# Sharing the start's PSUM copies between ScalarE and VectorE, with a new written-out order, in a Linformer attention and MLP-mixer kernel

## The chip, the cores and the metric

The kernel runs on one core of a Trainium2 chip. The metric is the device time of one execution in microseconds; each version is run several times and the median counts.

The engines are named as the profile does: PE (TensorE, with PEld for its weight loads), DVE (VectorE), ACT (ScalarE), POOL (GpSimd) and SP (SyncE). POOL, SP and ACT also have DMA queues (POOLq, SPq, ACTq). Line numbers (L510) are those of the kernel before.

## The reference

Eight batches, each with 8 heads, 1024 rows and 64 columns per head. Attention in the Linformer form is followed by an MLP mixer:

```python
k_proj = einsum('ks,bhsd->bhkd', E, k)          # 1024 rows of k to 64
v_proj = einsum('ks,bhsd->bhkd', F, v)
scores = q @ k_proj.T / 8
x = softmax(scores) @ v_proj                    # heads side by side: 1024 x 512 per batch
u = x + (relu(x.T @ w_tok1) @ w_tok2).T         # token MLP: 1024 -> 256 -> 1024
out = u + relu(u @ w_ch1) @ w_ch2               # channel MLP: 512 -> 1536 -> 512
```

All inputs and the output are float32.

## The kernel before, in words

**What one batch does.** The loads (`load_heads`, L344) bring pairs of heads of k, v and q from HBM through POOL's DMA queue, which casts them to bf16; the same queue brings the weights. `kv_proj` (L510) multiplies k and v by E and F on PE and copies the result out of PSUM (L523): two heads, four copies of 64x128. In batches 0 and 1 `k_transpose` (L550) turns the projected k on PE, and two copies (L561, L566) put it into `kT`; `q_transpose_pe` (L598) turns two heads of q, and one copy of 128x1024 (L606) puts them into `qT`. From batch 2 on these turns are DMA transposes in SP's queue: `q_transpose` (L579, two for a batch), `k_transpose_dma` (L533, from a tile `kb` that the copies of L523 fill), and `turn_u` (L776) for u. Then come the scores (L614), their exponentials on ACT (L623), the product with v (`attend`, L637), which also gives the sum of the exponentials, and the reciprocal (L649) and the product with it (L654) on DVE. That gives x.

**The MLPs.** The token MLP of batch 0 is `token1_part` (L1053) and `token2_part` (L1085); batch 1 has its own (L704, L728); from batch 2 on it is done with seven block products in place of eight (L868, L984). u of batch 0 is turned by PE (`u_transpose_pe`, L1114) with a copy. The channel MLP is done for 16 half-batches of 512 rows, also as seven block products each: `up_set` (L1173) makes the hidden values in three sets, `down_block` (L1282) brings them back; DVE and ACT form the sums of blocks between them. The results are added to u on DVE (L1322 and others), and `store` (L1316) sends them out. The last half-batch ends in `finish` with adds of 512 and 256 columns (L1364, L1372); only there the stores go through SP's and ACT's queues, otherwise through POOL's:

```python
queue = (nc.sync if sh else nc.scalar) if last else nc.gpsimd
```

**What sets the order.** Every piece of work is a job of a `Planner`. The order of all jobs is a string, `ORDER`: two characters name a job, and the jobs are issued one after the other as the string tells. `pin()` keeps each engine to that order, so an engine that waits for one job holds back all jobs behind it on the same engine, and a queue's DMAs start in this order. `SPOTS` gives each PSUM tile its bank. `FILLS` is a list of places in the order: for each entry a blank matmul of 128x512 on a zero tile (`blank(zero)`, L422) is put ahead of the PE job at that place.

```python
for place, j in enumerate(plan):
    if j.eng == "PE":
        for _ in range(FILLS.count(place)):
            blank(zero)
        pin()
```

Loads and DMA transposes are tied as well: they take turns where the code names it ("loads and transposes take turns"), so that a transpose isn't issued before the load that was put ahead of it.

Of the kernel before, what the change touches and what calls it, by code (L numbers as in the profile page):

```python
# [39 lines left out]
    "HCHrK0HtHLMxK1J-K2HIK4HMEeEiK3HAMzMwK5JyHuHwKCHNK6MyHxKDK7HJHvK9HGKHKFKAHyHzHKH+KGHOK8KJKEHHM+I0I1KK"  # L40
    "KBH-I8I2HPKLI3I9KOHQIAIEICHRKPHSKMKIIDHTM-N1KRIBIFHWN7N3HXN8IGI4N4KNIQNCIINDHUKTKUI6IHHYIRN9KVIJN5IK"
    "KSNAISIYNBKWHVILIMN6KZNEKXNHIZNFKbKaKcIOINNINGNJIVKdNRNSIWNKI7NLKeKfKjIXNMKhIbKgKkNNKnNOKYKlKiKmIaK-"
    "IcNPNQI5KoNTL0KQNWNXITNUL3NVLeIdNYIPIUKqIfNZKpKrL4KtL1NaNbKsLgIgIeN2N0QvNcL6KvNdIjKuNeL7L2KwLiL9IhNf"
    "NgLhLjL5LHNiNhL8LAIkLmNlLnNmLkQwLINjNkQxKxNnLpLBNoNqQzNpIlLJLCNrLqLfKzR1NsLPKyNvNtNwLDNzNuLQLoLFNxLs"
    "LEN+Q-LMR0IiLlLrQyNyO1LwLNHZO2N-K+LRO0LOO4O6LuO5LxLvLtL+LSO8O3O9O7LTLKLyQ+L-OAOBLUOGLzOCM1ODM2R2OEOI"
    "OHLLM0OJM4LVOKM5OLLGLaONM3MCOOOPMDLbLWMGOSOMOTRGMEOQRHLXLcOFOVLYMFMHRBR7OZR9M6OROXImM7RCR8MIRDRERAOa"
    "MJMURLObMKMMM8RFOYMLOdRIMAOcRMMNRJMORQMVRKMPOeMWLdLZR5OnRNOoOgOUROOWMQMSMcOrMdRPRRMRMeRVOpRSOhOjOqOs"
    "RTOkOfRUOiMZRXP3MaOlP4R4MBOuR6M9RWMbRYP5P6OvP7MfOmRZRcMgRaP8RdOxReMTOyPARbOtRfMhRgOwPiMXRhP9PmOzPBMY"
    "O+MjMiPDRiPCR3U+RjPkPEMnPLO-RkRlMkMlPnPFRpPqPMRnMoRmPGRoRqRrV1PNPrRsP1PHPtRuPoRtPuRvRzPTV5V3MpV4R+V2"
    "PJPjRwUzMmPsRxPUPIPpRyP+P0S5R-PvS1PVS2P-S6PlPQS3P2S0PyS8PRS9PzSAQ2PwS4SCS7Q0Q3SBSDSKPOSEPxQ5SLSHSFPK"  # L50
    "PSSISNSPQ6Q1PWQ8SOSGPXPPQGSMSRPYQ4PZPaSSQ9Q7V6U-PeSJV0STPbQHQKPcSWQASXSQPfQIQBQLPgQCQNQEQOQJV9VBSUQM"
    "V7VCVAV8QQQYQPSZQRVGSbQZSVVDVHQaSdQSVLVEVFQgVIQTQUQhVJVMSeVQQWVKVRMqSrSfQiSsVNShVVQdVOVPSaQXScSvVSPd"
    "StSgSiSjVTQDVUQVSwQeSySuVXSkQfVWQFSxSzVYQbSlS-VZVcS+VdVeQjSYSmSnT1TmT2QkVfSoSpVaQcT7VgToQlQnVhVbT0T8"
    "ViQoQmTnSqVjTpTBTqTDVkQpT9TCVpTEQrVlTrVnTATFVqVmTsTuVoVrTvTtVtQsTHT3TGQtTJVsVuTwVvTKTxVwTPTyVzTIVxT+"
    "V+VyTQW5PhQqT-TLW6TzV-W1TNT5TRQuW0TOW2U2W3U0WAU3TUU6W8TVU4TXW4W9WBTMT4U7TWWCW7WKTYU5U9TaWDWEU1UAWFTb"
    "U8WHUCWLTZWGWPWNUDWITSUKWOTcUBTTT6WRWMULUOUMUETeUPUNWSUQTdURTiTfWTUSWQUFUTWWWUWJUcUUTgWVWZWbWaTjWdUW"
    "UVTkWeUdUXUGUeWhWrWfUIUkWsWtWiWvUlWXUJUYWkUaWgUmWcWYWwWyWjX7WlWzUhWuThWmW-WpWnWqUiX8X0XDXBUjUHWoXCWx"
    "W+UnX9XEUoUZUfX1UgUpUbXFXAUrXGXqX2UqXmXJUsXPXHX3XKUvXoXLXNUtXrXsXuY6X5UwXtXIXQXvUuTlY7XRXxY8XnY9YAXy"
    "XXXwXYXMYBXpXOUxXZXzX4X6YDXUYOX+XVYEYPYQX-Y0YCXWYFYRUyXaXSY1YSXbYIYTXTY2XcYUYVYJYgXdYWXeYXXiYKYaY4YM"
    "YbXfXgYhYcXjYGYiYeYYYlYmXhYHYZYLY5Y3YNYfYdYnYwXkYkYoYpYjYqYrYzYtXlYsYuZ2Y+Z3YxYyZ4Z0Z6Y-Z7Z5YvZ1"  # L60
)
SPOTS = (
    "0216767372004241743211210031467364663002714006266137366770745014321020343451242142366575657675676667"
    "7557666576757656767765576102412401523203141541105557565676566757775665675764616706422432141243315012"
    "0141427567656565656666670736756201231505435511212012030665767656565656667360764741251524320415432152"
    "0321575666656665656666461563741340314535104120320312376576665656565666627367460403154103035254241214"
    "35776565656565656666471675605021042104541332150313467"
)
FILLS = (6, 11, 15, 15, 15, 15, 15, 15, 15, 18, 18, 30, 30, 30, 41, 41, 60, 60, 87, 87, 87)
# [19 lines left out]
HWK = 0  # L89
FMAX = 3.4028234663852886e38  # L90


class Job:


    def __init__(self, n, eng, occ, lat, fn, prio):
        self.n, self.eng, self.occ, self.lat, self.fn, self.prio = n, eng, occ, lat, fn, prio
        self.deps, self.next, self.takes, self.banks = set(), [], [], []
        self.start = self.end = None
        self.early = self.behind = False  # L100
        self.mms = 0

# [82 lines left out]
def kernel(  # L185
# [13 lines left out]
    nc = tc.nc  # L199
# [3 lines left out]
    KP = E.shape[0]  # L203
# [123 lines left out]

    def sp(t, fn, **kw):
        return pl.add("DMA", t, t + 2.0, fn, **kw)
# [158 lines left out]
    def kv_proj(b, h0, hn, due, block=False, apart=False):  # L488
# [9 lines left out]
        sides = {"k": (0, k_to, "kb" if block else "kp", ET_sb, k_sb), "v": (KP, v_to, "vb", FT_sb, v_sb)}  # L498

        def side(names):  # L500
            bk = Bank(stream[0], full=False)

            def view(n):
                at = sides[n][0]
                return bank(bk).rearrange("p (h d) -> p h d", d=D)[at : at + KP, 0:hn]

            def mm():
                for si in range(NSI):
                    for n in names:
                        nc.tensor.matmul(  # L510
                            view(n), sides[n][3][:, si, :], sides[n][4][:, hs, si, :],
                            start=(si == 0), stop=(si == NSI - 1),
                        )
# [5 lines left out]
            ).mms = NSI * len(names)  # L519
            for n in names:  # L520
                for i in ((0, 1) if n == "k" else (1, 0)):
                    act(
                        cols, lambda n=n, i=i: nc.scalar.copy(out=sides[n][1][i], in_=view(n)),  # L523
                        writes=[(sides[n][2], i, h) for h in heads], uses=[bk],
# [15 lines left out]
    def k_transpose(h0, hn, due):  # L540
# [7 lines left out]
        def mm():  # L548
# [11 lines left out]
        act(  # L560
            hn * KP, lambda: nc.scalar.copy(out=kT[0:D, hs, 0, :], in_=view()[0:D, 0:hn]),  # L561
            writes=[("kT", 0, h) for h in heads], uses=[bk],
        )
        act(
            hn * KP,
            lambda: nc.scalar.copy(out=kT[D : 2 * D, hs, 1, :], in_=view()[D : 2 * D, 0:hn]),  # L566
# [990 lines left out]
```

## Time and profile before

| | |
|---|---|
| median of 3 runs | 419.5 us (419.3 to 419.77) |
| the profiled execution: its time | 419.51 us |
| its span | 417.7 us (1.8 us of the time lie outside it) |
| mean granted TensorE clock | 0.999 |
| PE busy | 409.2 us, 98% |
| DVE busy | 356.8 us, 85% |
| ACT busy | 229.8 us, 55% |
| POOL busy | 66.7 us, 16% |
| HBM read, written | 59.24 MB, 16.78 MB |

The span is the time from the first to the last instruction or packet on the core. Busy time of PE counts pipelined matmuls from start to modelled end, so 100% busy says that there is always one in flight. The three longest groups of matmuls are L1173 and L1282, the channel MLP's two halves, and they fill most of the span; the chain that ended last is PE for 92%. Shares of busy time are means over the whole span, while the stages differ: the first 24 us load and project, the middle repeats one pattern per half-batch, and the last few us store.

A row of the timeline gives the start, the length of the group, the engine, line, operation, and the tiles out and in; brackets at its end give idle time before it and the work that ended this idle time.

### The profile page before, as it was taken

The numbers are of one execution on the slowest core, as the hardware profiler recorded it, in microseconds if no ns is written. First come the engines' busy times: TensorE is split into PE (matmuls) and PEld (weight loads), VectorE is DVE, ScalarE is ACT, GpSimd is POOL, SyncE is SP. The second block draws the span as 40 slices with busy tenths as digits, with TensorE's granted clock in tenths as the row PEclk, the third lists the DMA queues.
The fourth block names the chain that finished last, engine by engine and source line by source line (L and its number), as shares of the span: only waits on it lengthen the run. The fifth ranks groups of instructions, "written<-read, shape, count | busy, mean of one in ns | idle before, by whom it ended". The sixth has DMA issues, their size and how long they took to land.

```text
span 417.7 us, 9441 instructions
## 1 busy us (share of the span) xinstructions
PE 409.2 (98%) x3843; PEld 348.6 (83%) x3843; DVE 356.8 (85%) x760; ACT 229.8 (55%) x446; POOL 66.7 (16%) x105
## 2 busy tenths in 40 slices
PE   7999999999999999999999999999999999999995
PEld 3589888688888889889898888888798889988884
DVE  2288988999999898898989898998898997988684
ACT  2858984375746456565356645564545555362520
POOL 8544020013000220112001210112101000000100
PEclk9999999999999999999999999999999999999999
DMA  9999999996999888899948896396947411230314
GB/s 166 206 201 206 206 202 186 187 149 113 241 161 189 141 184 175 166 189 174 231 77 153 134 241 150 77 194 114 229 77 202 52 52 52 52 100 2 152 51 153
DMA packets 96812, 62.48 MB, mean 150 GB/s; under 512 B 62080, under 2 KB 92288, under 8 KB 96768
## 3 DMA queue, kind: packets, MB, share of 16 engines
q0 software_dynamic: 35088, 45.09, 54.7%
q1 hardware_dynamic: 61056, 16.00, 22.7%
q10 hardware_dynamic: 624, 0.79, 0.6%
q8 instruction: 30, 0.49, 0.5%
q14 instruction: 14, 0.11, 0.1%
HBM read 59.24 MB, written 16.78 MB: 182 GB/s over the span
## 4 chain that ended last, share of the span: by engine, by line
PE 92%; DMA 3%; ACT 2%; POOL 1%; issue 0%; DVE 0%; POOLq 0%
PE psum L1173 35%; PE psum L1282 34%; PE psum L868 4%; PE psum L984 4%; PE psum L510 3%; PE psum L614 3%; PE psum L673 2%; DMA k_sb<-in_k_dram 1%; DMA kT<-kb 1%; PE psum L637 1%; PE psum L1085 1%; PE psum L1053 1%; PE psum L704 1%; ACT qT L606 1%; PE psum L598 1%; PE psum L1114 0%
## 5 line engine op out<-in xcount | busy, mean ns | idle before, releaser
L1282 PEld LDWEIGHTS <-G 128*128 128x128 bf16 x1344 | 130.5, 98 | 16.8
L1282 PE MATMUL psum<-wc_sb,G 128*128 128x256 bf16 x768 | 103.8, 273 | 0.0
L1173 PEld LDWEIGHTS <-wc_sb 128*128 128x128 bf16 x768 | 73.9, 98 | 10.4 <-issue 0.4
L1282 PE MATMUL psum<-wT,G 128*128 128x256 bf16 x576 | 78.4, 273 | 0.0
L1195 ACT ACTIVATE G<-psum 128x512 bf16<-128x512 f32 x96 | 57.3, 600 | 36.3 <-PE psum L1173 36.2
L1209 DVE TENSOR_TENSOR G<-G 128x512 bf16<-128x512 bf16 (+1 forms) x140 | 69.7, 516 | 1.3 <-ACT a L623 0.5
L1173 PEld LDWEIGHTS <-wT 128*128 128x128 bf16 x576 | 55.5, 98 | 8.5 <-issue 1.0
L1173 PE MATMUL psum<-S,wc_sb 128*128 128x256 bf16 x384 | 57.1, 273 | 0.0
L1173 PE MATMUL psum<-uT,wc_sb 128*128 128x256 bf16 x384 | 56.6, 273 | 0.0
L1173 PE MATMUL psum<-S,wT 128*128 128x256 bf16 x384 | 56.1, 273 | 0.0
L1316 POOL DMA_DIRECT2D out_dram<-o x30 | 16.2, 543 | 204.1 <-DVE o L1322 139.0
L623 ACT ACTIVATE a<-psum 128x512 bf16<-128x512 f32 x64 | 37.2, 601 | 19.0 <-PE psum L614 18.9
L1322 DVE TENSOR_TENSOR o<-psum,u 128x512 f32<-128x512 f32 x59 | 40.4, 685 | 6.8 <-PE psum L1282 6.4
L1201 ACT COPY ub<-psum 128x512 f32<-128x512 f32 x48 | 28.2, 588 | 31.6 <-PE psum L1173 27.7
L1201 ACT COPY ua<-psum 128x512 f32<-128x512 f32 x48 | 28.2, 589 | 21.3 <-PE psum L1173 20.9
L1216 ACT COPY psum<-psum 128x512 f32<-128x512 f32 x48 | 27.8, 580 | 20.2 <-PE psum L1173 9.1
L1154 DVE CUSTOM_DVE_ANT_0 G<-psum,ua 128x512 bf16<-128x512 f32 x48 | 32.9, 685 | 5.3 <-PE psum L1173 2.7
L1154 DVE CUSTOM_DVE_ANT_0 G<-psum,ub 128x512 bf16<-128x512 f32 x48 | 32.9, 686 | 4.8 <-PE psum L1173 4.3
L344 POOL DMA_DIRECT2D v_sb<-in_v_dram x18 | 13.4, 746 | 103.4 <-DMA uT<-u 51.8
L1173 PE MATMUL psum<-uT,wT 128*128 128x256 bf16 x192 | 28.8, 273 | 0.0
L690 DVE TENSOR_TENSOR x_sb<-psum,rdn 128x512 bf16<-128x512 f32 x40 | 27.6, 689 | 0.9
L614 PE MATMUL psum<-qT,kT 128*128 128x512 bf16 x64 | 22.1, 380 | 0.3
(106 smaller groups left out, 546.1 us busy)
## 6 DMA issues: line engine op xcount, KB each, us to landing
out_dram<-o POOLq DMA_DIRECT2D x30, 512.0 KB, 4.5
v_sb<-in_v_dram POOLq DMA_DIRECT2D x14, 512.0 KB, 6.6
k_sb<-in_k_dram POOLq DMA_DIRECT2D x14, 512.0 KB, 8.7
q_sb<-in_q_dram POOLq DMA_DIRECT2D x14, 512.0 KB, 11.4
wc_sb<-in_moe_w_ch_dram POOLq DMA_DIRECT2D x6, 256.0 KB, 12.1
wc_sb<-in_moe_w_ch_dram POOLq DMA_DIRECT2D x4, 384.0 KB, 13.6
k_sb<-in_k_dram POOLq DMA_DIRECT2D x4, 256.0 KB, 7.1
v_sb<-in_v_dram POOLq DMA_DIRECT2D x4, 256.0 KB, 7.0
```

The source lines that it names most:

```text
L614: lambda: nc.tensor.matmul(bank(bk), kT[:, h].rearrange("p c k -> p (c k)"), qT[:, h].rearrange("p j s -> p (j s)"), start=True, stop=True,),
L623: lambda: nc.scalar.activation(out=a_t[h // 2 % 2][:, h % 2], in_=bank(bk), func=ACT.Exp, scale=scale),
L690: lambda: nc.vector.tensor_tensor(out=x_sb[:, :, h * D : (h + 1) * D].rearrange("p (n c) d -> p n c d", n=2), in0=view()[:, :, :, 0:D], in ...
L868: nc.tensor.matmul(to, tok1_of(n, si), mv, start=(n == 1 and si == 0), stop=(si == NJ - 1), skip_group_check=True,)
L1154: nc.vector._custom_dve(TENSOR_ADD_SAT, out=out, in0=in0, in1=in1, s0=FMAX, s1=0.0)
L1173: nc.tensor.matmul(t[:, c, :], w1_of(n, dd, 2 * m + c), a_of(j, n, dd), start=(n in (1, 7) and c == 0 and dd == 0), stop=(c == 1 and dd == 1),
L1195: lambda: nc.scalar.activation(out=G[:, n, cs], in_=view(src), func=ACT.Relu),
L1201: 512, lambda: nc.scalar.copy(out=dst, in_=view("y")), writes=[(name, s % 2)],
L1209: 512 * len(both), lambda: f(out=G[:, n, c], in0=G[:, a, c], in1=G[:, b, c]), ps=False,
L1216: 512, lambda: nc.scalar.copy(out=view("y"), in_=view("x")), takes=[bk["y"]],
L1282: nc.tensor.matmul(to, G[:, G_OF[n], cc, t * P : (t + 1) * P], w2_of(n, cc), start=(n in opens and (t == 0 or alone) and cc == 0), stop=(c ...
L1322: 512, lambda: nc.vector.tensor_add(out=dst, in0=view(src), in1=u_of(sh, dh)),
```

## The change

**Copies.** A helper `copy()` issues a PSUM copy to ACT or to DVE. 29 units of copies (those of a `kv_proj` call, of a `k_transpose`, a `q_transpose_pe` or a `u_transpose_pe` in batches 0 and 1) take their engine from a string `SIDES`, one character each. Five are D: unit 0 (k and v of heads 0 and 1 of batch 0: four copies of 64x128), unit 5 (q of heads 2 and 3: one copy of 128x1024), unit 7 (kT of heads 4 and 5: two copies of 64x128), and in batch 1 unit 22 (kT of heads 0 to 3: two copies of 64x256) and unit 24 (q of heads 2 and 3: one of 128x1024). These ten copies go from ACT to DVE.

```diff
+SIDES = "DAAAADADAAAAAAAAAAAAAADADAAAA"
...
+    sides = iter(enumerate(SIDES + "A" * 99))
+
+    def copy(unit, cols, dst, src, **kw):
+        n, engine = unit
+        if engine == "D":
+            j = dve(cols, lambda: nc.vector.tensor_copy(out=dst, in_=src()), **kw)
+        else:
+            j = act(cols, lambda: nc.scalar.copy(out=dst, in_=src()), **kw)
+        j.unit, j.cols = n, cols
+
+    def scalar():
+        return None, "A"
...
+            unit = scalar() if block else next(sides)
             for n in names:
                 for i in ((0, 1) if n == "k" else (1, 0)):
-                    act(
-                        cols, lambda n=n, i=i: nc.scalar.copy(out=sides[n][1][i], in_=view(n)),
-                        writes=[(sides[n][2], i, h) for h in heads], uses=[bk],
+                    copy(
+                        unit, cols, of[n][1][i], lambda n=n: view(n),
+                        writes=[(of[n][2], i, h) for h in heads], uses=[bk],
                     )
...
+        unit = next(sides)
+        for c in range(2):
+            rows = slice(c * D, (c + 1) * D)
+            copy(
+                unit, hn * KP, kT[rows, hs, c, :], lambda rows=rows: view()[rows, 0:hn],
+                writes=[("kT", c, h) for h in heads], uses=[bk],
+            )
...
-        act(
-            1024, lambda: nc.scalar.copy(out=qT[:, 2 * hp : 2 * hp + 2], in_=view()),
+        copy(
+            next(sides), 1024, qT[:, 2 * hp : 2 * hp + 2], view,
...
-        act(
-            512, lambda: nc.scalar.copy(out=uT_t[i][:, :, hp, :], in_=view()),
+        copy(
+            next(sides), 512, uT_t[i][:, :, hp, :], view,
```

**Order.** `ORDER`, `SPOTS` and `FILLS` are new throughout; the matmuls of the jobs are the same, and the blank matmuls go from 21 to 15.

```diff
-FILLS = (6, 11, 15, 15, 15, 15, 15, 15, 15, 18, 18, 30, 30, 30, 41, 41, 60, 60, 87, 87, 87)
+FILLS = (7, 14, 14, 14, 14, 14, 14, 14, 15, 20, 20, 33, 58, 58, 77)
```

What the new order moves, read from the strings:

- The loads of batch 0 (the number is the pair of heads): before k01, v01, v23, q01, k23, q23, q45, k67, k45, v45, q67, v67; after k01, v23, v01, k23, q01, k67, q23, q45, k45, v45, q67, v67.
- The loads behind them: before v, wc2, wc2, k, wc2, wc2, q; after k, v, then four of wc2, then q.
- On PE two score matmuls that stood ahead of the projection of batch 0's v67 stand behind it. Eight matmuls of `token2_part` move from ahead of the first matmul of L1173 to behind it, and four of `u_transpose_pe` from behind to ahead.
- Batch 2: before, the copies of one projection on ACT were vb, kb, kb, vb; after, kb, kb, vb, vb. Its loads were v, v, k, q, k, q, and are q, v, k, k, q, v. The first store of output was issued some time after them, and is now the next in POOL's queue behind them. SP's order is unchanged: q, q, k, u.
- The end: SP's queue had the last block's row t=1 (the output of the last add), then row t=0, then the store of the other 256 columns; it now has these 256 columns, row t=0, row t=1. ACT's queue had the store of the first add and then that of L1364; it now has them the other way round.

More of the change, by code (lines that the diff above doesn't have):

```diff
@@ new lines @@
+    "1A1S0C1D141p1T2A1g1B181E1Q2B2C1i1F1C151h1k1R1j1a19161b1l2D1n1m1U1c1d1V2E1s1X1q271t1e1r2F0D211W1+1Y1f"
+    "29282H1u0E2G1Z222I1-231v201x2a0F2b1w2V2M2W2J2P1y2S2c2X1z2f2Y2K2Q2R0I0H0G0J2Z2L2g2d2h2k2N2i2O2T2e2U2l"
+    "2t2m2p2j2u2n2q332x342r2o2y2-2v3B302z3C2s2w2+0K35313T320c0Y3U3Q360Z3P0a3l3J373D3R3V3E3W0d0e383K3Z410b"
+    "0N0M0L3m3X3Y3F3p3G393a0O3q3n0g3S3b3c3o3s0h3t3H3r3L3d3f420i3v3A3g3u0f3e3I4h0j4543474k4648443w3x504g49"
+    "3y5x51524A4D4l4m4B4i3h5y5-4E4j534o5z4n4p4C0k4J545+4K3z4F3j4r60564L4s3-554R4H0o0l4u620p57580q614G0m63"
@@ new lines @@
+    "593N4S65645A6N5B666O6P5C4O6R5D4P3i4T6S6Z4q3M676a4Q6Q6W6e6A4U5I3k3+4t696X404I4w686B0n6Y6C6D6E4M6T4V4v"
+    "6f6g5E5J6b3O6U6V6F4N6H6G5M6hAH6I6i4W6c0r5F6d4Y6j6L5G6K4x5N6m4X6k6l4Z6p5K6u6q5P6r4a5Q5L6J6v6n5O6w6s6o"
+    "6tAI4c6x6z6M735a6y5R70745S6+6-A9787571725T5b7B79765U7A7K777H7C5c4dAK5H7LAJ7I7D5i7J7E7N7M7F4y7G5V5W7Q"
+    "7O7R7PAL4+7S5YABAA4-7TAC4e4z7V7U7W5j5X7X5f7Z5gAMANAOAQAP7Y7a5h7e7f4b7c7b7gAT5d7d5l7hAVAXAW7i5mAY5kAh"
+    "7j5Z5nAiAZAb5eAj7pAcAdAa81Ak7l7nAeAmAf7qAnAoAlAg5p7r7t7sAu7u5q827mAvAxAp5oAy7oAw7w85AzB05rA+AqB183Ar"
@@ new lines @@
+    "7vA-86B27x7yAs885tAtBBB5B6B7847-7zB880BCBDB3897+B98J87BEBF8BASBA8ABGB48KBJBM8L8D8N8CBHBKBIBNBL8EBP8M"
+    "8OBSBQBTBRBUBO8P8b7k8Q5u8RBZ8TBVBX8cBWBY8SAU8yBa8UBb90BcBdBe91Bf8+5v8V8W94BgBj959E8FAD8X8zBk92AR9FBh"
+    "Bi979G9HBl9I98EnBn8-8HAF9AEjEk4fBm8Z93Br8d9JBsEr9BEpEq9L8jBo8GAEBp9MBuBwEo8k8Y96AGBvByEs8gBxBt999OBz"
+    "Bq5s9WB+C4B-9C9P8lElC08h9XC59a9D8iC1C2C38eC79Y8m9K8aC88n8I9N9ZC68oC9CB8f9Q9bCC8p9R9dCE9cCD8q8uCG9e9g"
+    "8rCN9hCA9fE-Cb8vCF9iCHExCJCOF0CLEzEyCREvE+8s8wEmF4F59oCSF19pCP5w9S9jCM9qCUF2CVF9F3CQCcF69w9k9UCK8tF7"
@@ new lines @@
+    "F8CX9xFA9l9yFBCdCYCfFECtCTFC9mFDFG9tCeFFFOCICuEw9VCvFHFICWCg9u9vFPCxCZCiFJ9zCwFLFKDW9TCa9+CjFM9rCyCz"
+    "FNEuEt9n9-DYFQFRChFS9sC+FTCkFUFVClC-CnD0A1D1A0FWCmD2DXDaD3IoFXFYDbA2CoA5FZD4D9FdDcFbFeDeDdFfA3CpFcFg"
+    "IrA4InDfFiCqFaIvFjDhFhDiDZFkD5IsDAA6DBD7A7CrD6ItFlFnFmDkFoFpFvDlFrFqFsFwDgDHDjFtIuFxF+DoFyF-FzDpDmDn"
+    "CsG8DE8xA8G0FuG1D8DsDFIpIwDqG2DGDtG9DrDIDvE4G5DwG3DJG4DKDyG6GBDLDuGDGAE5GCDMG7E8DxGEDzDCGFD+DOGGDDE9"
+    "DPD-GHGKEBGIDNJ8J9DQGLEAGRGJE0J3J1ECEDE6DSJ4GSE7I-EGJ0EEIqEHGNJ2GPDTEFGTEMDUJ5GUGVJ6GWJ7GOENJDE1GQJA"
@@ new lines @@
+    "GYIzGfGMEOEIJBEUGZJCEKGgJEGbEVJFE2JGJIJHEWGjGcERJJJKJLGkGXJSJTJMGmGlDRGhESEJGaHbGnETJPGpJQGdGiJRGoGx"
+    "JNEXJUGeJVJWELJOGyEYEPE3EZGzJXJYG-EQG+JZGqH0HeGrHaEbJaGsEcHcH2HfHiH1HjJbHdEaJcHgJhEdJdHlH3JeJfJgHmJi"
+    "EfH5EgJjJlH6HhJkH4HkJmHDHnJnH7HqEhH8JrJoHEJpJsHsJqGtHoJvHtHpJzGuH9HrJ+HFJtDVMsIxIyMrI+EeMvJuHBJwHAJx"
+    "K2K0HwHCHLHuJ-JyK1MtMxMzHxK3HzK4GvK5KCMuHMHIHvH+KDI0K6HNGwMyMwK9I1KAM+K7HJKFKGK8I8KHHGKJKEHKHHI9KKHO"
+    "HyKIKLICIAKOH-IDHPKPIBIFKMKBN7N3I2IGHQIIHSHRN4KNI3N8NCN5HTKVIEN6IJKSKRN9KWI4HWHUKTIHIQNAIKKXIRKUNBNE"
@@ new lines @@
+    "ILIMNDNFISKZHXNHNGKaKYIOI6NJHYIYKbIVINN1I5NKKcHVEiIZIWNLIaIXIPNINMKjNOKdNPKfKkHZNQIbKlKQI7KgNNKeKmNT"
+    "ITNWKnKhNUNVNXKoNYIcLeNRKiNSIUKqK-IdNZIfKrL0NaNbNcKtKpL3NdNeL1IgIeN2KsLfKvNfL2L4LHL6NgNlKwNhLIKuM-N0"
+    "QwNjIhL7L9IjNkLgL5NmIkLiQyL8NiIiNnLBNpNoNqLCNrLALDLELFKxKzLjLJQzNsNvLPLmNwQ+Q-LnR1IlNtLQLMLpLkNuR0Ll"
+    "O1LqLGKyLRNxLoLwK+NzN+LNNyN-O3O2LhR2O4O6LrLOO5LxLyL+LuO7O0O8O9LvL-LsLSOAM1LTOBLzM2OCODQvOGM4OHLKOJLL"
+    "OEOILtM5LUImMCOKQxLVONOOM0MDOLLWOPMGMHOMLaM3OSRBOQLXOTORLYRCRGRHR7OFOVM6LbMJMELcR8MIRDR9OZMFM7MKOaMU"
@@ new lines @@
+    "OXREMMM8RAOWRFMLOdObMVMOMNOeOYMAR4R5RLRIOcMPRJMWOnRKOUOgMcMQRMOoRNLZR6MSOhR3MdOrOjM9RVMZMTRORPRSRWMe"
+    "OpMaRTOsRUP3LdUzMbOuRXRQRYMBOqRZMfOfMgOkP4OvRaP5OiRROxOlMRRbRcMXP7MhPiRdOmReP8MjOtP6RfRgMkPAMYOyPmRh"
+    "OwPjMiRiOzRjPBPDPEMnPLMoPnRkPkMlRlP9PqPlO+RpPCO-RnRoPrRqV1PFRmRrPMPGV2V3RsU+PNPtRuPHP1PoPuRvMpRtRwPs"
+    "RzPJPTP2PpRxR+V5PUP+RyV4R-S5PvV6U-V0S1PyS2PVS0P-S3P0Q0PIPwS6S8PzS9SAMmPQSKQ2SBS4SCPRS7PxQ3SLSDQ1QGPS"
+    "Q5SFQ6SEPWSNSHQHSGQ8PKSIQ4SPQ9SOPXPOSRSMPPQ7PYSSQKQIQAQLSTSWQJSQPaQNSUQOPbSXPZQBV7SVSJVGVBPeSZQMV8VH"
@@ new lines @@
+    "VDPcQPQYQQVCVEPfVFQCSbV9QSVLPgQTQRVAQZVMVISaSdSrVQQaSeQgVRVJVKVNMqShSfVVQhSiQUQEVOSgVPPdVSQWQFSsVTSY"
+    "QiQdSkQeSlVWVUSvVXSxSjQVQfVYQDStSwVZQjSySmVcScVdTmSuSpSqQkSzQbT7SnSoQXT8VeS+VfQcQlVgT1QnVhQmT2ToVaTB"
+    "T9T3QoVbTCViS-T0TATqTEQpVjVkVlQrTDT4TFTrVpVqQsVnVmTuTvVrTsQtTHTxVoVtTGVsTnVuTITyVvTtT5TJTwVwVzU2VxTP"
+    "TKTpPhQuU3TLV+TzU6VyQqU4V-W1U7W2TNTMW3W0W5U5TQU9W6WAU0TRUAW8T+WBW9W7TUU1WCT-TXU8TVUCWDWFWETWUDWGW4UK"
+    "TYULTSWKWHTaTZTOUBUOWLT6WITbWNUEWMTTUPURTcWOTdWRWSWPTeUFUMTfTiUNWQUSUQTjUUUcWTUGWJUVTgUTWZWdUWWUWWWr"
@@ L64 @@
[L64 to L67, printed above, removed]
+    "2724114217403233244062631342166077027031640162031764367273645204310510123414223420467676657656777655"
+    "6755676755677565656565766130210231205534414313030775566775667575556777567570757627420142215235410152"
@@ L68 @@
+    "1421256766656565656566665546706300431403413410234502120767667656565656666270672640431543143551254401"
+    "2035577665656565656667260762734112104303124521052032166566765656566666617076474051435051343203520502"
+    "15767567656565676666474761734550332404245132135010467"
 )
[L69 removed]
+FILLS = (7, 14, 14, 14, 14, 14, 14, 14, 15, 20, 20, 33, 58, 58, 77)
 WHOLE = 3
@@ L101, in __init__ @@
         self.mms = 0
+        self.unit = None
 class Bank:
@@ L497, in kv_proj @@
         v_to = [vb[i * KP : (i + 1) * KP, hs, i, 0:D] for i in range(2)]
-        sides = {"k": (0, k_to, "kb" if block else "kp", ET_sb, k_sb), "v": (KP, v_to, "vb", FT_sb, v_sb)}
+        of = {"k": (0, k_to, "kb" if block else "kp", ET_sb, k_sb), "v": (KP, v_to, "vb", FT_sb, v_sb)}
         def side(names):
@@ L510, in mm @@
                         nc.tensor.matmul(
-                            view(n), sides[n][3][:, si, :], sides[n][4][:, hs, si, :],
+                            view(n), of[n][3][:, si, :], of[n][4][:, hs, si, :],
                             start=(si == 0), stop=(si == NSI - 1),
@@ L559, in k_transpose @@
         )
-        act(
-            hn * KP, lambda: nc.scalar.copy(out=kT[0:D, hs, 0, :], in_=view()[0:D, 0:hn]),
-            writes=[("kT", 0, h) for h in heads], uses=[bk],
-        )
-        act(
-            hn * KP,
-            lambda: nc.scalar.copy(out=kT[D : 2 * D, hs, 1, :], in_=view()[D : 2 * D, 0:hn]),
-            writes=[("kT", 1, h) for h in heads], uses=[bk],
-        )
+        unit = next(sides)
[5 more added lines that the diff above has]
+            )
     turned_u, rest = {}, {}
```

55 lines of the change are left out of this document (6 added, 49 removed).

## The prediction

> **What bounds the kernel now.** I read the page's busy table first, then the table of windows, then the waits, the chain and the timeline where a window showed a gap. Line numbers are those of the kernel before.
>
> ```profile
> span 417.7 us, 9441 instructions
> PE 409.2 (98%) x3843; PEld 348.6 (83%) x3843; DVE 356.8 (85%) x760; ACT 229.8 (55%) x446; POOL 66.7 (16%) x105
> 12.00:14.00 2.00, 2.00 (x21) 0.97 (x16) 0.00 (x0) 1.72 (x6) 0.88 (x2) 1.00 1.23 203
> 16.00:18.00 2.00, 1.68 (x15) 0.86 (x17) 0.00 (x0) 2.00 (x5) 1.13 (x2) 1.00 1.23 203
> 20.00:22.00 2.00, 1.91 (x14) 0.84 (x13) 1.65 (x7) 1.96 (x5) 0.55 (x2) 1.00 1.14 210
> 24.00:26.00 2.00, 2.00 (x39) 2.00 (x37) 1.97 (x9) 0.40 (x1) 0.74 (x1) 1.00 1.26 197
> 100.00:150.00 50.00, 50.00 (x466) 43.74 (x464) 47.20 (x96) 27.75 (x54) 8.00 (x13) 1.00 1.04 184
> ```
>
> The columns behind the length are busy time of PE, PEld, DVE, ACT and POOL, then granted clock, DMA share and GB/s. From 24 us on PE has work without a gap (50.00 of 50 us). A time can change in three places only: ahead of 24 us, at a wait inside the full part, and behind the last matmul. Ahead of 24 us ACT is the full engine (2.00 and 1.96 of 2 us) and DVE is empty until 18; PE's weight loads fill under half. So the span is a start that ACT and the loads set, then PE's work, then a tail.
>
> ```profile
> 20.75 0.10 PEld L614 LDWEIGHTS <-kT 128*128 128x128 bf16 x1 [0.48 <-ACT kT L566]
> 22.30 0.63 PE L510 MATMUL psum<-v_sb,EFT_sb 128*64 128x128 bf16 x8
> L344 POOL DMA_DIRECT2D v_sb<-in_v_dram x1: 718/718/718, 10.5 to 10.5; - x1
> DMA to landing us min/median/max: 10.9/10.9/10.9
> ```
>
> These are the timeline, and the issue of the v load for heads 6 and 7. The v data, the last input that batch 0 needs, landed at 10.5 + 10.9 = 21.4. Its projection on PE (L510) began at 22.30, 0.9 later, because PE is in order and what stood ahead of it had waited for ACT's kT copies. PE is full behind it.
>
> **The start.** Five of the 29 copy units go to DVE. In batch 0 that takes from ACT four 64x128 copies at 0.262 (L523), one 128x1024 at 1.012 (L606) and two 64x128 at 0.260 (L561, L566): 1.05 + 1.01 + 0.52 = 2.6 us. ACT was full there, so what waits for ACT comes earlier, up to the next limit: the last v load. It keeps its place among the twelve loads, which only change places, so it lands at 21.4 again. A load that landed at 11.48 had its first matmul at 11.53; so the last projection can begin at 21.42 instead of 22.30: -0.88. The order has two score matmuls less ahead of this projection; they are done behind it and cost 2 x 0.216 = 0.43 there. Sure is then -0.45. Behind 22.3 PE lost another 0.15 to 0.27 in small waits, part of which ACT's lead removes; I take **-0.6**, ends -0.45 and -0.86. Two loads cap it: the third wc2 load lands at 45.37 and the first down products need it at work that PE reached at 46.0 (0.6 to spare); batch 1's q lands at 49.82 for work reached at 50.49. Nothing beyond 0.6 gets past 50 us unless these come earlier; their queue is full, 1.14 to 1.26 in the DMA column of the windows above.
>
> The copies' price on DVE is in no row. A 128x512 eviction on DVE took 0.69 (L451), a 128x256 one 0.42 (L654), a 128x4 one 0.18 (L649): by a straight line 0.30 for 64x128 and 1.23 for 128x1024 (ends 0.26 and 0.42; 0.69 and 1.4). Six and one make 3.0 us, at most 3.9. DVE idles 7.3 us before 14.5 and 3.9 before 19.0, so I cost them at nothing; behind such a copy only reciprocals and products of attend (L649, L654) are queued on DVE, which wait for the same heads anyway. Without that cover one 1.2 us copy would hold attend's outputs, and the token products that read them, for 1.2 us. Batch 1's three copies (two 64x256, one 128x1024; 2.1 us) come near 50 us, where PE waits for neither engine: nothing, 2.1 at worst.
>
> Six blank matmuls go (L422, 6 x 0.217 = 1.3 us). Each stood ahead of a job that waited, so what goes is filler time: nothing, or -0.2 where one delayed its job. The reordered PE jobs of the full part are the same matmuls: nothing.
>
> **The wait at 83 us.**
>
> ```profile
> 77.33 0.58 ACT kb L523
> 77.92 0.58 ACT kb L523
> 78.53 5.10 DMA kT<-kb
> 83.68 0.60 PE psum L614 x2
> ...
> DMA packets 600, 0.60 MB, mean 199 GB/s; under 512 B 16, under 2 KB 600, under 8 KB 600
> q0 software_dynamic: 600, 0.60, 122.7%
> qT<-q_sb SPq DMA_TRANSPOSE x1, 8.6
> ```
>
> First the chain of waits: batch 2's scores waited for the transpose of kb, 5.10 us from issue to landing; 0.38 of it stopped PE (83.30 to 83.68). Then the DMA view of 69 to 72 us: a transpose was issued at 69.00, and all 600 packets belong to queue 0, the loads; transposes moved only once it was empty, at 72.8. In the changed kernel the kb copies go ahead of the vb copies on ACT (1.2 us earlier), the k loads sit earlier, and the first out store (data ready near 64) is queued right behind the last load instead of at 74.56, where it lay among the transposes until 81.5. On SP the order stays qT, qT, kT, uT. Sum: queue empty 72.8, the store 0.524 MB at 0.39 MB/us (rate at 205 to 206) 1.3, so 74.1; two qT of 2.8 and 2.5 (undisturbed ones): 79.4; kT 1.25 and 0.6 to land: **81.3**. The upper end is 83.6, as before. By its matmul list PE wants it 0.2 us earlier in its work, and with the start's 0.6 at 82.5. Midway, 82.45, leaves about 0.1 of the 0.38: **-0.3**, ends -0.38 and +0.7. uT behind it lands at 84.3 to 84.7 (u ready at 80.0, 4.24 to 4.64 in quiet cases) for use at about 85.2: no wait, half a microsecond of cover.
>
> A rule is the other way. The Trainium skill, "DMA: Bandwidth & Descriptors", section "Queues, rings and completion order", says each DMA engine takes turns between its queues packet by packet. By that rule the transposes would share with the store and kT lands like before; the rows at 69 to 72 disagree, those at 78 to 81.5, where packets interleaved, agree.
>
> **The tail.**
>
> ```profile
> 411.52 1.69 ACTq L1316 DMA_DIRECT2D out_dram<-o  x2
> 412.76 0.42 DVE L1372 TENSOR_TENSOR o<-psum,o 128x256 f32<-128x256 f32 x1
> 413.21 1.35 SPq L1316 DMA_DIRECT2D out_dram<-o  x3
> 414.00:415.00 1.00, 0.00 (x0) 0.00 (x0) 0.00 (x0) 0.00 (x0) 0.00 (x0) 1.00 1.04 339
> ```
>
> SP's first store waits for the last add (L1372, to 413.2), and two stores whose data is ready before (409.8, 411.9) stand behind it, issued at 413.63 and 414.12; the last landed at 416.74. About 786 KB leave at 340 GB/s at the very end. In the changed order SP stores the 262 KB piece (ready 409.8) and the t=0 row (131 KB) first, and only t=1 waits. On ACT the two 262 KB stores are swapped against their data: the one ready at 411.5 now stands behind the one ready at 412.8. The burst is 786 - 393 + 262 = 655 KB: 131 / 340 = **-0.4**. Ends: -1.3 if one store issued at 413.2 lands in 2.20 (the quickest of SP's three) and is the last; 0 if the burst's length is not in its bytes. No row speaks for a loss, as nothing is issued later than 414.12.
>
> **Sum.** -0.6 - 0.3 - 0.4 = -1.3. Against the profiled execution's 419.5 (span 417.7, 1.8 outside it), which is the median of the runs too: **418.2**. The likeliest case's own range is 417.3 to 418.7.
>
> **Rivals.**
> *The gain is eaten at 83 us.* If kT lands at 83.6 again, PE only arrives earlier and waits longer; start and wait together give nothing, and the tail alone remains: 419.1, or 419.5 without it. For it: the interleaved packets of 78 to 81.5, and the store that is put ahead of the transposes. Against it: the 1.2 us that kb is earlier. Chance 0.25.
> *The clock falls.* Six blanks less leave PE emptier between 8 and 22 us. The price is in the first blanks:
>
> ```profile
> 0.99 1.03 PE L422 MATMUL psum<-zero 128*128 128x512 bf16 x2 [0.99 <-DVE zero L299]
> 8.12 1.69 PE L422 MATMUL psum<-zero 128*128 128x512 bf16 x7
> ```
>
> Two blanks in a row begin 0.40 apart at the opening (2 in 1.03 us with a 0.6 us tail), 0.217 at 8 us; the slow pace held until about 4.7 us, 3.8 us in all, so one fall costs 3.8 x (1 - 0.217/0.40) = 1.7 us, two 3.4. From 418.2 that is 419.9 to 421.6: slower at its middle, 420.8. It decides if the filling of 16 to 18, the emptiest window, falls by two blanks from 1.68 to 1.25 of 2 us and the clock does not bear it. Against it: that window had 1.00, with gaps under 0.5 us. Chance 0.10. The Trainium skill, "TensorE: Matmul & The Clock Gate", section "A second HAM failure mode: psum-queue depth-cycling", reports a kernel whose short idles between matmul groups made the clock swing; this trace, at 0.999 with such idles, does not show it so far.
> *A later stall.* The order is new everywhere, and a bank or transpose that comes late behind 90 us would stop PE; before there is none. One of 2.5 us gives 420.7. For it: DVE is 94% busy there (47.20 of 50). Against it: the same work in the same time per batch. Chance 0.07.
> *It does not do what it says:* ACT's swapped stores. It is inside the tail's ends.
>
> **How the numbers follow.** The forecast 0.58; eaten gain 0.25; clock 0.10; later stall 0.07. About 0.2% (0.84 us) is what a measurement of this kernel can tell from no change, so faster means under 418.7: the forecast's range, 0.58. The eaten gain is the same, 0.25; clock and stall are slower, 0.17. The range that leaves 2 in 10 out goes from the low end of the sum, 417.3, over the eaten gain to the mildest fall of the clock: 420.1.
>
> **What would show it.** Right: the last v projection at 21.4, the first up product near 31.2 instead of 32.0 (0.6, and 0.2 to 0.3 of token matmuls that its order puts behind it), clock 1.00 in all windows from 8 us, kT landed by 82.5, last matmul near 411.5, SP's stores issued one by one with the last at 412.3, span near 416.4. Wrong: a projection past 22, a wait for DVE in front of a PE instruction before 24 us, a wait of 1 us or more at 82 to 84, a granted clock under 1, any PE gap behind 90.

## The result, and the profile after

The changed kernel took 418.94 us in the median of 22 runs (418.33 to 420.4), the kernel before 419.81 (419.08 to 422.54). The ratio on record is 0.9972, 95% interval 0.9959 to 0.9984: faster by 0.28%, or 1.2 us. The two medians alone give 0.9979, or 0.9 us.

The profiled execution lost 1.1 us of span, 416.6 against 417.7. First the page's head and the table of windows (columns as before: length, busy time of PE, PEld, DVE, ACT, POOL, granted clock, DMA share, GB/s):

```profile
span 416.6 us, 9427 instructions
12.00:14.00 2.00, 1.33 (x15) 0.85 (x13) 0.00 (x0) 1.67 (x5) 0.92 (x2) 1.00 1.24 205
16.00:18.00 2.00, 1.66 (x15) 0.80 (x15) 1.46 (x7) 1.91 (x4) 1.16 (x2) 1.00 1.26 211
20.00:22.00 2.00, 1.80 (x23) 1.42 (x24) 1.43 (x8) 1.43 (x3) 1.08 (x2) 1.00 1.13 211
100.00:150.00 50.00, 49.98 (x464) 43.38 (x463) 46.74 (x97) 28.77 (x55) 6.88 (x11) 1.00 1.03 184
```

ACT has room at 20 to 22 us (1.43 in place of 1.96), DVE works where it was empty (1.46 at 16 to 18), PE has more idle time (it has six blanks less), and the clock is the same. Next the start's timeline and the issue of the last v load (lines shift: L525 is the old L510, L651 the old L637; the copies now carry the helper's lines, L335 on DVE and L337 on ACT):

```profile
20.14 0.62 PE L612 MATMUL psum<-ident,q_sb 128*128 128x128 bf16 x8 [0.76 <-DMA q_sb<-in_q_dram]
20.80 1.01 ACT L337 COPY qT<-psum 128x1024 bf16<-128x1024 bf16 x1 [0.57 <-PE psum L612]
21.47 0.63 PE L525 MATMUL psum<-v_sb,EFT_sb 128*64 128x128 bf16 x8
22.36 0.23 PEld L651 LDWEIGHTS <-a 128*128 128x128 bf16 x4 [0.24 <-ACT a L637]
22.85 0.23 PEld L651 LDWEIGHTS <-a 128*128 128x128 bf16 x4 [0.21 <-ACT a L637]
...
L359 POOL DMA_DIRECT2D v_sb<-in_v_dram x1: 716/716/716, 10.5 to 10.5; - x1
DMA to landing us min/median/max: 10.9/10.9/10.9
```

The v load landed at 21.4 as before, and its projection began at 21.47, not 22.30. Two things are new. Ahead of the projection PE now waits 0.76 us for the load of q heads 6 and 7, which it turns first. Behind it, twice PE waits for an exponential, which ACT makes after the copy of q heads 6 and 7. Then batch 2's transpose and the chain:

```profile
L549 SPq DMA_TRANSPOSE kT<-kb x1: 1352/1352/1352, 77.6 to 77.6; - x1
DMA to landing us min/median/max: 3.3/3.3/3.3
```

```profile
82.77 0.43 PE psum L628 x2
```

kT landed at 80.8; the scores at 82.77 follow PE's own work without a wait. Last the tail:

```profile
409.59 3.28 SPq L1330 DMA_DIRECT2D out_dram<-o  x3
412.08 0.42 DVE L1386 TENSOR_TENSOR o<-psum,o 128x256 f32<-128x256 f32 x1
412.15 0.92 ACTq L1330 DMA_DIRECT2D out_dram<-o  x2
```

SP's stores go out one by one from 409.6. ACT's two stores start only behind the 512-column add; the one whose data had been ready at 410.8 was issued second, at 412.58, and landed last of all, at 415.63.

From one profile to the next the same loads land up to 1.4 us apart, so stretches are compared, not times of day. In us; a star marks a granted clock under 1.00 in the start:

| kernel | v load lands | projection behind it | to the first up product | from there to the last matmul | last add's end to last landing |
|---|---|---|---|---|---|
| before | 21.37 | 0.93 | 9.72 | 380.42 | 3.55 |
| before, second profile | 21.49 | 1.41 | 9.71 | 380.09 | 3.54 |
| before, kb first | 22.09 | 1.06 | 9.68 | 380.07 | 3.55 |
| before, store late | 21.22 | 1.24 | 9.73 | 386.54 | 3.56 |
| before's order, copies shared * | 21.82 | 3.20 | 9.79 | 379.90 | 3.56 |
| changed | 21.37 | 0.09 | 10.07 | 380.23 | 3.13 |
| changed, ACT's stores in data order | 21.40 | 0.17 | 10.10 | 380.23 | 2.82 |
| changed, tail as before | 21.37 | 0.10 | 10.12 | 380.22 | 3.86 |
| changed, one blank * | 20.78 | 0.73 | 10.06 | 380.33 | 3.12 |
| changed, all on ACT * | 21.11 | 3.42 | 9.71 | 380.98 | 3.15 |
| changed, batch 1 on ACT | 21.66 | 0.10 | 10.09 | 380.95 | 3.53 |
| changed, vb first | 21.53 | 0.75 | 10.10 | 380.23 | 3.11 |
| changed, q67 on DVE * | 21.84 | 0.64 | 9.69 | 380.22 | 3.12 |
| the last but with the stores in data order | 21.43 | 0.26 | 9.66 | 380.23 | 2.41 |

Between the two orders 0.27 us of PE work changes sides of the first up product (eight matmuls of `token2_part` at 0.062 go behind it, four of `u_transpose_pe` at 0.056 ahead). At equal work the third stretch is 0.27 longer and the fourth 0.27 shorter in the changed order than the table says. So the pair's 1.1 us are 0.21 ahead of the first up product, 0.46 from there to the last matmul and 0.42 in the tail.

The table measures the projection from the v load, but another load holds it in the new order. The load of q heads 6 and 7 landed at 20.10 in the changed kernel; PE turned these heads, worked on without a gap, and began the projection 1.37 us after that landing. In all six profiles of the new order without a star this distance is 1.37, while the distance from the v load goes from 0.09 to 0.75. The run "vb first" tells the two loads apart: v landed at 21.53, q at 20.91, and the projection kept to q.

```profile
20.96 0.62 PE L612 MATMUL psum<-ident,q_sb 128*128 128x128 bf16 x8 [0.55 <-DMA q_sb<-in_q_dram]
22.28 0.63 PE L525 MATMUL psum<-v_sb,EFT_sb 128*64 128x128 bf16 x8
```

### The profile page after: what moved, and what is told of

It reads as the page before. It is cut to its first block, busy times and chain, and to the rows that moved or that the text cites. A ratio compares the mean times of both kernels' runs of the same rounds, so it can differ in the third digit from the quotient of the medians.

```text
span 416.6 us, 9427 instructions
## 1 busy us (share of the span) xinstructions
PE 407.9 (98%) x3829; PEld 348.3 (84%) x3837; DVE 359.1 (86%) x770; ACT 228.9 (55%) x436; POOL 66.7 (16%) x105
## 4 chain that ended last, share of the span: by engine, by line
PE 92%; DMA 3%; POOL 2%; ACT 1%; DVE 1%; issue 0%; POOLq 0%
PE psum L1187 35%; PE psum L1296 35%; PE psum L998 4%; PE psum L882 4%; PE psum L525 3%; PE psum L628 3%; DMA q_sb<-in_q_dram 3%; PE psum L687 2%; PE psum L651 1%; PE psum L1099 1%; PE psum L1067 1%; PE psum L718 1%; PE psum L742 1%; POOL k_sb L359 1%; PE psum L612 1%; POOL q_sb L359 1%
## 5 line engine op out<-in xcount | busy, mean ns | idle before, releaser
L637 ACT ACTIVATE a<-psum 128x512 bf16<-128x512 f32 x64 | 36.7, 597 | 25.5 <-PE psum L628 21.3
L628 PE MATMUL psum<-qT,kT 128*128 128x512 bf16 x58 | 20.5, 379 | 0.1
```

The lines of the kernel that those rows point to most:

```text
L628: lambda: nc.tensor.matmul(bank(bk), kT[:, h].rearrange("p c k -> p (c k)"), qT[:, h].rearrange("p j s -> p (j s)"), start=True, stop=True,),
L637: lambda: nc.scalar.activation(out=a_t[h // 2 % 2][:, h % 2], in_=bank(bk), func=ACT.Exp, scale=scale),
```

## The experiments

**The copies and the order apart.** Two kernels complete a square.

```diff
-SIDES = "DAAAADADAAAAAAAAAAAAAADADAAAA"
+SIDES = "AAAAAAAAAAAAAAAAAAAAAAAAAAAAA"
```

> The changed kernel's order with all 29 copy units on ACT. Theory (ACT's 2.6 us of relief lets the last v projection start when its load lands): without it the projection of v heads 6 and 7 slips from 21.47 to 22.3 or later, and what follows it on ACT slips too; span +0.5 to +1.5. Rival (the new order and the new order of the loads did it, the copies are beside the path): projection by 21.7, span +0.0 to +0.2.

```diff
 SIDES as in the changed kernel
-ORDER, SPOTS, FILLS of the changed kernel
+ORDER, SPOTS, FILLS of the kernel before
```

> The order, banks and blank matmuls of the kernel before, with the five copy units on DVE: the copies alone. Theory (ACT's relief frees the start): the projection of v heads 6 and 7 goes from 22.30 to 21.5 to 21.9, as the old order has two score matmuls more ahead of it, the wait at 83 us grows or stays, span 417.0 to 417.5 against 417.7. Rival (the copies pay only with an order that is made for them): projection at 22.2 to 22.4, span 417.6 to 417.8.

| ratio to the kernel before | copies on ACT | five units on DVE |
|---|---|---|
| old order | 1 | 1.0011 (0.9996 to 1.0027) |
| new order | 1.0053 (1.0033 to 1.0073) | 0.9972 (0.9959 to 0.9984) |

Neither part gains alone; the new order without the copies loses 0.5%. With all copies on ACT the projection came 3.42 behind its load, more than the theory had. The windows and waits of that run show ACT full and PE empty (the rows of PEld and PE see the same two waits):

```profile
16.00:18.00 2.00, 0.73 (x10) 0.56 (x10) 0.00 (x0) 1.94 (x6) 1.30 (x2) 1.00 1.24 204
18.00:20.00 2.00, 1.68 (x12) 0.85 (x11) 0.98 (x5) 1.99 (x5) 0.74 (x1) 0.65 1.26 210
```

```profile
PEld L651 <- ACT a L637: 2.7, 2, 2.2
PE psum L651 <- ACT a L637: 2.3, 2, 2.0
```

The copies alone did not bring the projection to 21.5: it began 3.2 behind its load, after one wait for DVE's kT copies (1.28 us in PEld's row, 1.02 in PE's). The timeline of that run shows why:

```profile
22.74 0.42 DVE L668 TENSOR_TENSOR x_sb<-psum,rdn 128x256 bf16<-128x256 f32 x1
23.08 0.58 DVE L335 CAST kT<-psum 64x128 bf16<-64x128 f32 x2
23.71 0.10 PEld L628 LDWEIGHTS <-kT 128*128 128x128 bf16 x1 [1.28 <-DVE kT L335]
```

In the old order the copies stand behind attend's products, while the scores (L628) wait for them. My theory of this run was wrong and its rival right. The clock had fallen as well (0.50 at 14 to 16 us), and this execution, 421.86 us, is one of two of ten near 421.9; the other eight took 419.8 to 420.6. So part of the 3.2 belongs to the execution and not to the copies. No run takes the new order apart beyond batch 2's copies, the tail and the blanks: what its new order of loads is worth alone stays open.

**Batch 1's copies.**

```diff
-SIDES = "DAAAADADAAAAAAAAAAAAAADADAAAA"
+SIDES = "DAAAADADAAAAAAAAAAAAAAAAAAAAA"
```

> The changed kernel with batch 1's three copies (kT of heads 0 to 3, q of heads 2 and 3) on ACT again and batch 0's on DVE. Theory of the prediction (these are beside the path): PE waits for no copy between 45 and 60 and works there as in the changed kernel. Rival, from the run with all copies on ACT (PE waited 0.7 and 0.5 at 45 to 60): these copies hold PE there, 0.5 to 0.8 more idle time of PE in 40 to 60 us.

```profile
PEld L1296 <- issue: 0.7, 1, 0.7
PE psum L628 <- ACT a L637: 0.5, 1, 0.5
```

The rival. These waits at 40 to 60 us are absent from the changed kernel, and the stretch to the last matmul was 380.95, 0.72 longer than in the changed kernel. The run with all copies on ACT has the same (380.98). The two rows are one stop of PE, at 54.69, and each kernel has one profile here.

**The blanks and the clock.**

```diff
-FILLS = (7, 14, 14, 14, 14, 14, 14, 14, 15, 20, 20, 33, 58, 58, 77)
+FILLS = (7,)
```

> The changed kernel with one blank matmul in place of 15 in the start (14 x 0.217 = 3.0 us less PE work before 20 us). Theory (the blanks keep the granted clock, and the change came close to losing it): PE runs slow for a time in 8 to 22 us, granted clock under 1 there, two neighbouring 128x512 matmuls 0.4 apart in place of 0.217, span +1.7 to +3.4. Rival (the clock holds with the loads' own matmuls): clock 1.00 and span within 0.2 of the changed kernel, perhaps 0.1 better.

```profile
8.00:10.00 2.00, 0.64 (x15) 0.47 (x15) 0.05 (x1) 0.00 (x0) 2.00 (x4) 0.91 1.20 188
10.00:12.00 2.00, 1.07 (x16) 0.82 (x15) 1.02 (x4) 0.43 (x3) 1.03 (x3) 0.50 1.16 183
```

The clock did fall, to 0.50 from 10 to 16 us; eight transposes of q took 1.04 there, 0.62 in the changed kernel. The mean granted clock of all nine runs is 0.988 to 0.992, so it fell in each. But the price was far under the theory's: the ratio was 0.9975 (0.9966 to 0.9985), which isn't told from 0.9972. The projection began at 21.52, against 21.47 in the changed kernel; it stood 0.73 behind its load, but that load had landed 0.6 earlier, so the 0.73 isn't shown to be the clock's. PE waits for loads in this stretch anyway; that slow matmuls use up this time is my reading, not a measurement.

**The wait at 83 us.**

```diff
 ORDER of the kernel before (two characters a job; 4b is the first store of output)
-AY 4b 5e Aj Ai 7b AZ Aa Ab 7p 5n AC 7q 81 Ae 5p AT 7l
+AY 5e Aj Ai 7b AZ Aa Ab 7p 5n AC 7q 81 Ae 5p AT 4b 7l
```

> The kernel before with the first store of output put behind the next load in POOL's queue, so that it isn't among batch 2's transposes. Theory (its packets among the transposes made kT late): kT lands 3.0 to 3.3 after its issue at 78.5, so by 82, and PE's wait of 0.38 at 83.3 is gone. Rival (kT was late because the kb copies came late or the q transposes ahead of it were long): kT's issue and the wait stay as they were.

kT landed 3.04 after its issue at 78.66 and no wait was left, as the theory had it. The move cost 6 us elsewhere: the store now landed at 93.89, and until then an add (L1332) could not write into its tile, which made PE wait 4.7 us further on. Behind this wait the granted clock fell to 0.50, from 95.9 to 99.3 us. Two rows of the waits and one of the windows:

```profile
DVE o L1332 <- DMA out_dram<-o: 5.0, 1, 5.0
PE psum L1173 <- DVE S L799: 4.7, 1, 4.7
96.00:98.00 2.00, 2.00 (x12) 1.51 (x11) 1.97 (x7) 0.00 (x0) 0.00 (x0) 0.50 0.97 211
```

```diff
 ORDER of the kernel before (AM, AN: kb copies; AP, AO: vb copies)
-AP 5j 7W 5X 7T 7X AM 7U AN 7Y AO
+AM AN AP 5j 7W 5X 7T 7X 7U 7Y AO
```

> The kernel before with the two kb copies of batch 2 ahead of the vb copies on ACT. Theory (the store among the transposes is the cause): kb is ready 0.6 earlier, but SP is busy issuing the q transposes until 78.43, so kT is issued 0.1 earlier at most and PE still waits 0.25 to 0.4 at 83.3. Rival (late kb copies are the cause): the wait is gone.

The wait was gone, against my theory. But the whole start of this execution was 0.8 later, so PE came to the scores at 84.19, and kT landed 3.28 after its issue at 78.70. A second profile of the kernel before itself changed the question:

> The kernel before once more, for a second profile: the loads landed up to 0.9 us earlier or later from one execution to the next. What belongs to the kernel recurs: the last v projection 0.9 to 1.1 behind its load's landing, PE's wait for kT of 0.2 to 0.4 near 83, the last landing 3.5 to 3.6 behind the last add. What belongs to that execution does not.

```profile
L533 SPq DMA_TRANSPOSE kT<-kb x1: 1231/1231/1231, 79.1 to 79.1; - x1
DMA to landing us min/median/max: 3.6/3.6/3.6
```

What I expected to recur did so for the start (1.41, more than my 0.9 to 1.1) and the tail (3.54), not for this wait: kT took 3.6 us in place of 5.1, and PE did not wait. The 0.38 belonged to one execution. That the wait was absent from the two single runs above therefore shows no cause, neither the store's nor the copies'.

```diff
 ORDER of the changed kernel
-AM AN AO AQ AP
+AO AP AM AN AQ
```

> The changed kernel with batch 2's vb copies ahead of its kb copies on ACT. Theory (the store ahead of the transposes gave the time): kT is issued at 78.7 in place of 77.55 and lands 3.3 later, at 82.0, still ahead of the 82.77 at which PE wants it: no wait. Rival (the order of the kb copies took the wait away): PE waits for kT, 0.2 or more, at 82 to 84.

kT was issued at 79.60 and landed at 82.75, and PE did not wait; this execution ran 0.8 later from the start, so PE came to the scores at 83.46. With the vb copies first the new order has no wait either.

**The tail.**

```diff
 ORDER of the changed kernel (Y-, Z1: ACT's two stores; Yv, Z5, Z7: SP's three)
-Yy Z4 Y+ Z0 Z1 Z3 Yv Z5 Z6 Y- Xl Z7
+Yy Z4 Y+ Z0 Z3 Z6 Xl Y- Z7 Z5 Yv Z1
```

> The changed kernel with the five stores of the last half-batch in the order of the kernel before (SP: row t=1, row t=0, the 256 columns; ACT: first add, then that of the 512-column add). Theory (the share of the tail in the gain is the later burst): the last landing goes back from 3.13 us behind the last add to 3.56, span 417.0, +0.4. Rival (the tail's gain came from elsewhere, for example from the last adds): span 416.6 as it is.

Span 417.4, last landing 3.86 behind the last add, ratio 0.998 (0.9963 to 0.9996). By these profiles the order of the stores is worth 0.43 to 0.73 us, by the medians of the runs 0.37 (419.31 against 418.94), and the two intervals overlap. Its size isn't settled: with the changed kernel's stores in the changed kernel's order the run with batch 1 on ACT has 3.53 in the table, and two profiles of one and the same end further down have 2.82 and 2.41. Why it is 3.86 here and 3.54 to 3.56 in all profiles of the old order stays open.

```diff
 ORDER of the changed kernel
-Yy Z4 Y+ Z0 Z1 Z3 Yv Z5 Z6 Y- Xl Z7
+Yy Y- Z4 Y+ Z0 Z1 Z3 Yv Z5 Z6 Xl Z7
```

> The changed kernel with ACT's last two stores in the order in which their data comes. In the changed kernel's trace the store put behind the other (256 columns by two rows, 262 KB, data ready at 410.8) is issued at 412.58 and lands last, at 415.63; SP's last store lands at 414.75. Theory (the queue order holds a ready store back, and that store ends the kernel): it is issued near 410.8 and lands near 413.2, SP's last 131 KB then end the kernel at 414.4 to 414.8, span 415.4 to 415.8 instead of 416.6. Rival (the end is a fixed latency behind the last add, whatever is queued): last landing stays near 415.6, span 416.5 to 416.7.

The early store landed at 413.23, and SP's last store ended the kernel; but that store took 2.79 us to land in place of 2.22, so only 0.3 of the expected 0.8 to 1.2 came: 2.82 behind the last add, span 416.4, ratio 0.9964 (0.9952 to 0.9977), not told from the changed kernel's.

**One more copy on DVE, and both edits.**

```diff
-SIDES = "DAAAADADAAAAAAAAAAAAAADADAAAA"
+SIDES = "DAAAADADAAAADAAAAAAAAADADAAAA"
```

> The changed kernel with one more copy on DVE: that of q heads 6 and 7 (128x1024; 1.01 us on ACT at 20.80, 0.68 on DVE). In the changed kernel PE waited 1.0 us in all for the exponentials between 22 and 24, and ACT does this copy ahead of them. Theory (this copy is what holds the exponentials): they start 0.4 to 0.5 earlier, the first up product comes 0.2 to 0.5 earlier than 31.53, span 416.1 to 416.4. Rival (DVE's reciprocals and products queue behind the copy and hold the token products): first up product at 31.5 or later, span 416.6 to 417.

The stretch from the projection to the first up product was 9.69 in place of 10.07, as the theory had it, and one wait of 0.2 for an exponential was left. The span, 417.4, was no better: the v load landed 0.5 later, and the clock had fallen to 0.50 at 12 to 14 us, though up to 20 us this program is that of the changed kernel. Ratio 0.9969 (0.9957 to 0.9981), not told from the changed kernel's.

> The changed kernel with ACT's last two stores in the order of their data and the copy of q heads 6 and 7 on DVE: both edits that shortened a stretch. From the two runs apart: the last landing came 2.79 behind the last store's issue and 2.37 behind the last add's end in the first (3.13 in the changed kernel), and the stretch from the last v projection to the first up product was 9.70 in the second (10.07). If they add up: first up product 9.6 to 9.8 behind the projection, span end 0.2 to 0.5 earlier behind the last matmul than in the changed kernel, ratio to the kernel before 0.9945 to 0.9965. Rival (either only moved a wait): ratio as the changed kernel's, 0.997.

Both edits together: 417.59 us, ratio 0.9947 (0.9933 to 0.996), span 415.7. First up product 9.66 behind the projection, last landing 2.41 behind the last add (2.82 in the run with the same stores, so 0.4 of it is one execution against another). All five runs, 417.46 to 417.91, lie under the fastest of the changed kernel's 22, 418.33: this version beats both kernels.

## Why the prediction was right or wrong, by its own steps

The sum was -1.3 and the ratio gives -1.2 (-0.7 to -1.7); the forecast case, a gain, came about. The time itself, 418.94, lies above that case's own range (417.3 to 418.7), as the kernel before also took 0.3 more than in its first three runs. The terms hold less well than the sum: at equal work the pair gives -0.21, -0.46 and -0.42 for the forecast -0.6, -0.3 and -0.4. That a start sized too large and a middle sized too small partly cancel is luck.

**The start (-0.6).** Right: with ACT's relief the projection came 0.83 earlier, and two scores went behind it. Right by luck: the place, 21.47 for the predicted 21.42. The prediction named the last v load as the next limit; it was the load of q heads 6 and 7, which landed 1.37 us ahead of the projection in every profile of the new order without a star, and in the first of them this came to 0.09 behind the v load. In "vb first" it came to 0.75. Wrong: "small waits, part of which ACT's lead removes". New waits came there instead, for exponentials queued behind the copy of q heads 6 and 7; the run with that copy on DVE took them away (10.07 to 9.69). In the profiled pair the first up product came 0.48 earlier, 0.21 at equal work, a third of the 0.6. Over all profiles without a star the old order's projection stood 0.93 to 1.41 behind its load (mean 1.16) and the new one's 0.09 to 0.75 (mean 0.25), so the 0.84 of the pair is typical.

**The wait at 83 (-0.3).** This step failed. The 5.10 us of kT were taken for a property of the kernel; a second profile has 3.6 and no wait. In the pair the stretch to the last matmul did shrink by 0.19, 0.46 at equal work, so the number looked right, by luck; against the second profile the same stretch is 0.14 longer, 0.13 shorter at equal work. My sum for the landing, 81.3 (it was 80.8), was good, but little was to be gained. Two readings in it were off. Transposes did not move "only once it was empty, at 72.8": in the profile before their first packets came at 72.04, with 169 load packets still to come until 73.80, so the rows of 69 to 72 don't show that a transpose waits for an empty queue. And the reordering of ACT's copies gives kb 0.6, not 1.2, as one vb copy stood ahead; with the earlier start, kT was issued 1.0 earlier. By the sum's own numbers kT at 82.45 would meet a PE that comes at 82.5: the 0.1 that it leaves is a hedge.

**The tail (-0.4).** It measured 3.13 against 3.55 in the pair, with a spread of 0.4 between profiles of one and the same end, and the store swapped against its data landed last, as its issue time said.

**What was costed at nothing.** On DVE the copies did cost PE nothing: none of PE's waits between 8 and 60 us in the changed kernel names a copy on DVE. But the prediction priced only what stands behind a copy. The run with the old order showed the other side: a copy that stands behind attend's products comes late itself. The price of 128x1024 was at its lower end, 0.69 and not 1.23:

```profile
14.82 0.69 DVE L335 COPY qT<-psum 128x1024 bf16<-128x1024 bf16 x1 [3.94 <-PE psum L612]
19.43 0.59 DVE L335 CAST kT<-psum 64x128 bf16<-64x128 f32 x2 [0.19 <-PE psum L566]
```

The 64x128 copies took 0.30, as estimated. The Trainium skill, "VectorE: DVE Perf Modes", section "Why PSUM operands drop a tier", has it that a PSUM source caps 2-byte data at twice the rate of 4-byte data; the trace agrees, as 1024 bf16 columns took what 512 f32 columns did (0.69). I had drawn my line through f32 rows alone.

The copies' worth was mis-sized further: I read from before that ACT's relief frees 0.9 us in batch 0 and nothing in batch 1. In the new order, without them, the first up product came 13.1 us behind the v load's landing instead of 10.2, and 0.75 was lost behind it. The clock fell in that profile too, but the one run of the four with a mean clock of 1.000 took 421.01, still 2.1 above the changed kernel. The profiles of the old order are free of these waits in batch 1.

**The rivals.** The clock's mechanism is there: 0.50 without the blanks, and in the start of three profiles with them. The price of 1.7 us holds where PE has no other idle time: the run with the late store lost 6.1 to 6.5 us in the stretch behind the first up product, 4.65 of it in the wait, which leaves 1.5 to 1.8 for a fall of 3.4 us. In the start, where PE waits anyway, the run with one blank had the clock down for 6.8 us and no loss that its ratio can tell. The changed kernel itself isn't free of the rival: 4 of its 22 runs have a mean granted clock of 0.995 or 0.996 and took 419.5 to 420.4, the other 18 took 418.3 to 419.6. Among the fourteen profiles the five with a fall ahead of the last matmul have 0.991 to 0.996 and the other nine 0.997 to 1.000; these four runs left no profile, so a fall is likely there and not shown.

PE's longest gaps ahead of the four falls in the start were 1.2, 1.3, 1.6 and 2.0 us, the one ahead of the fifth 4.65. The Trainium skill, "TensorE: Matmul & The Clock Gate", section "What's actually happening", gives one idle window of about 3.4 us for it; the fifth fall agrees, the four in the start came without such a gap, so there the measurement decides.

The eaten gain did not come, and no later stall: the stretch behind the first up product was 380.22 to 380.23 in six of the profiles.

## What to carry to other kernels

Moving work to an idle engine and writing a new order are one change: each alone lost or gained nothing here, because an engine that is kept to its order serves a moved copy only as early as its place in the program. When a start comes where it was forecast, look for an execution in which the candidates for its release lie apart: here the v load and the q load did so clearly in one profile only. Before a wait from one profile goes into a sum, see it in a second profile, and measure distances from the load or event that starts a stretch rather than times. In a queue that ends a kernel, put ready stores ahead of waiting ones on every queue: the one that was left the other way round was the last to land (0.3 us in the profiles, too little for the runs to tell).

## What the runs showed of the hardware

Ahead of the last matmul the granted clock fell to 0.50 in five of fourteen profiles. Four falls are in the start, each after a stretch of 2 us in which PE was busy for 0.81 us or less; one profile had 0.55 and no fall. The fifth came behind a gap of 4.65 us. Each lasted 3.41 us, the one in the run with one blank twice that (6.83). One program can have a fall in one execution and not in another: the mean clock of the ten runs with the copies alone is 0.995 to 1.000. The load queue's landings shift by up to 1.4 us between profiles with the same loads: that of q heads 6 and 7 came between 19.55 and 20.91 in the new order.
